# Block products by sevens in a fused attention and feed-forward kernel: the first feed-forward product computed over two token tiles with seven block products, and its rounds re-dealt

## The chip, the cores and the metric

One core of one Trainium2 chip runs the whole program. The metric is device time in microseconds (us); three runs of the kernel before gave 860.07, 860.36 and 865.73 us, so the median is 860.36 us. Everything is float32.

## What is computed

An attention block in which only scores close to the row's maximum survive, and a feed-forward block behind it. Cut to what matters:

```python
# q, k, v: (8 batches, 8 heads, 576 tokens, 64)
scores = q @ k.T / 8
scores = where(scores >= max(scores) - tau, scores, -1e9)
attn   = exp(scores - max) ; attn = attn / (sum(attn) + 1e-9)
x      = heads side by side of (attn @ v)          # (4608 tokens, 512)

h      = x @ w_in                                  # (4608, 1024), "first product"
e      = exp(h - max(h)) ; solu = h * e / (sum(e) + 1e-9)
ln     = (solu - mean) / sqrt(var + 1e-6) * g_ln
out    = ln @ w_out                                # (4608, 512), "second product"
```

## The kernel before, in words

**Slots and rounds.** The attention part is cut into 144 slots (`slots`, `NS`), 18 for each of the 8 batches (`PER`). A slot is 128 query rows of each head of a pair of heads against all 576 keys. Per batch, 16 slots belong to kinds 0 and 1 (four pairs of heads, two slots each) and two to kind 2, the last 64 tokens of each head. One pass of the big `while` loop is a round. Round n issues slot n's scores and, behind them, the later steps of earlier slots and pieces of the feed-forward part. The order of all instructions is written out by hand (`manual_schedule`), so each engine runs its own list strictly in the order in which the program emits it.

**A slot's steps.** `scores` (L472, TensorE) fills two score tiles in PSUM, `s0` and `s1`, with one buffer each: round n+1 can only write them when round n has been read. `maxes` (L494, VectorE) takes the row maxima from PSUM, one instruction for each head. `ramp` (L509, ScalarE) reads the scores from PSUM a last time and writes `w` in SBUF. `exps` (L518, ScalarE) exponentiates `w` and sums it. One round later `normalise` (L525, L526, L528, GpSimd) divides `w`, and `blocks` (L540, VectorE) transposes it into `T` in 32x32 blocks; after two slots DMAs rearrange `T` into `wT` (L549 to L556). Three rounds after the second slot of a pair of heads, `attend_steps` (L582, TensorE) multiplies `wT` with v into a PSUM tile `pv`, and `attended` (L614, ScalarE) copies it into the token tiles `xh` (or `xe` for kind 2).

**A token tile's steps.** When a kind's four pairs of heads are done, two tiles of 128 tokens are ready; kind 2 gives one tile for every two batches, 36 tiles in all. `ff_h` (L647, in the drain after the last slot L637) does the first product in two parts in two rounds, into one PSUM tile `h_ps`, 64 matmul instructions of 64x512 for a tile as the profile counts them. The array is used as four 64x64 quarters at once. Where the row half that adds into a bank changes, a `fence` (L108, a GpSimd memset that waits for TensorE, and that the next matmul waits for) keeps the two apart. Then come `ff_max` (L662, VectorE), `ff_exp` (L671, ScalarE), `ff_mul` (L677, VectorE), `ff_sum` (GpSimd), `ff_stats` (L692 and L693 VectorE, then five small GpSimd instructions L696 to L703), `ff_norm` (L713, ScalarE), `ff_norm2` (L718, VectorE), `ff_swap` (four DMAs, L729), `ff_turn` (L739, VectorE, a transpose into `uT`), and `ff_o` (L752, TensorE, again in two parts in two rounds) into a PSUM tile `o_ps`, copied out by `ff_out` (L767, ScalarE) and stored by `ff_store`.

**PSUM.** Eight banks: the two score tiles hold four, and the other four are two tiles `p0` and `p1`, which `take` hands out by turns to `pv`, `h_ps` and `o_ps`. A product with v and the two feed-forward products thus never share a bank.

**Order in steady state.** A tile's first product takes two rounds, each with a product with v if one is due, and the second product of the tile before takes the next two rounds, without one. While a slot's scores are with VectorE and ScalarE, TensorE works on these. For batches 2 and up q and k arrive untransposed, are scaled by GpSimd, transposed by VectorE (`turn_natural`, L212, called "flip" here) and rearranged by DMA. Within one round a list `begin` runs before the scores, `middle` after `normalise`, and `late` after `blocks`.

Of the kernel before, what the change touches and what calls it, by code (L numbers as in the profile page):

```python
# [8 lines left out]
F32 = mybir.dt.float32  # L9
# [11 lines left out]
def kernel(  # L21
# [61 lines left out]
    seed = const.tile([P, 1], F32, name="seed")  # L83

# [7 lines left out]
    natural = {}  # L92
    ends = {}
# [27 lines left out]
    def load_one(b, hf, nm, queue=None):  # L121
        d = halves.setdefault((b, hf), {})
        hs = slice(4 * hf, 4 * hf + 4)
        src, rows = {"q": (q, ROWS[0]), "k": (k, ROWS[1])}[nm]
        d[nm] = loads.tile([P, 4, 4, D], F32, tag=nm, name=nm)

        parts = [slice(0, 2), slice(2, 4)] if b == 0 and hf == 0 else [slice(0, 4)]
        for x, part in enumerate(parts):
            queue = nc.scalar if nm == "k" and x + 1 < len(parts) else nc.sync
            queue.dma_start(  # L130
                out=d[nm][:, part].rearrange("p h t d -> p h (t d)"),
                in_=src[b, hs, 0:SM, :][part].rearrange("h (p t) d -> p h (t d)", t=4),
            )
            if hf == 0 and x == 0:
                if b not in ends:
                    ends[b] = loads.tile([P, H, D], F32, tag="ends", name="ends")
                load_ends(b, nm, slice(0, 2) if len(parts) > 1 else slice(0, H), queue)
# [6 lines left out]

    def load_qk(b, hf):
        load_one(b, hf, "q")
        load_one(b, hf, "k")
# [43 lines left out]
    def load_natural(i, nm, a):  # L191
        raw = loads.tile([P, 4, 4, D], F32, tag=nm, name=nm)
        natural[i, nm, a] = raw = raw.rearrange("p h t d -> p (h t d)")[:, 0 : NK * D]
        nc.sync.dma_start(out=raw, in_=qk_rows[nm][a, 64 * i : 64 * i + P])
# [69 lines left out]
    def weight_load(x):  # L264
        raw = work.tile(
            [P, 512], I64 if wide else F32, tag=("xh2", "xh3", "uT", "xh1")[x % 4 if x < 15 else 0],
# [9 lines left out]
    def weight_a(x):  # L276

        if not wide:
# [3 lines left out]
            work.tile([P, 512], I32, tag=t, bufs=n, name="em") for t, n in (("ob", 2), ("xe", 1))  # L282
# [68 lines left out]
    def pair(i):  # L351
        if i not in pairs:
            qT = heads.tile([P, S], F32, tag="qT", bufs=6, name="qT")
            pairs[i] = dict(
                qT=qT[:, 0:SM] if i < 2 * NP else qT,
                kT=heads.tile([P, S], F32, tag="kT", name="kT"),
                qe=heads.tile([P, ST], F32, tag="qe", name="qe"),
            )
        return pairs[i]

    def q_item(i, ts=slice(0, 4)):
        src, h0 = source(i)
# [3 lines left out]
        def make(spare, x):  # L366
            for t in range(n):
                turn(
                    spare, x + t, lambda r, y: src["q"][ROWS[r], h0 + y, ts.start + t], swap=True
# [19 lines left out]
    def k_item(i, ts=slice(0, 4)):  # L389
        src, h0 = source(i)  # L390
# [3 lines left out]
        def make(spare, x):  # L394
            for t in range(n):
                turn(spare, x + t, lambda r, y: src["k"][ROWS[r], h0 + y, ts.start + t])
# [9 lines left out]
    def e_item(i):  # L406
        src, h0 = source(i)
# [152 lines left out]
    def attend_steps(key):  # L560
# [3 lines left out]
        unit["y"] = take("pv")  # L564
# [3 lines left out]
        for e in range(2) if kind == 2 else [None]:  # L568
            for m in range(NK):
                for u in range(2):  # L570
                    d, h0 = source(b * NP + (hp if e is None else e + 2 * u))
                    for h in range(2):
# [4 lines left out]
                        else:  # L577
# [11 lines left out]
                            start=m == 0, stop=m == NK - 1,  # L589
# [3 lines left out]
    def attended(key):  # L593
# [13 lines left out]
        else:  # L607
            if hp == 0:
                xh[b, kind] = work.tile(
                    [P, NP, 256], F32, tag=f"xh{(2 * b + kind) % 4}", bufs=1, name="xh"  # L610
# [4 lines left out]
        pairs_free.append(tag)  # L615


# [46 lines left out]
    def ff_exp(t):  # L664
        d = ffn[t]

        starts.append(t)
        tag = "xh1" if rnd > NS and len(starts) % 2 else "u"
        d["u"] = work.tile([P, DFF], F32, tag=tag, bufs=1, name="u")
# [5 lines left out]
    def ff_mul(t):  # L675
        d = ffn[t]
        nc.vector.tensor_tensor(out=d["u"], in0=d["h"], in1=d["u"], op=ALU.mult)  # L677
        pairs_free.append(d["tag"])
# [65 lines left out]
    def ff_o(t, part):  # L744
        d = ffn[t]
        other = len(t) == 3 and t[0] > 1 and t[2]
        if part == 0:
            d["otag"], d["o"] = take("o_ps")
        for m in range(NC * part, NC * part + NC):
            for r in range(2):  # L750
                for z in range(2):
                    nc.tensor.matmul(  # L752
# [331 lines left out]
```

## Time and profile before

| | |
|---|---|
| median of three runs | 860.36 us |
| the profiled execution's own time | 864.95 us |
| its span | 863.2 us |
| granted TensorE clock, mean | 0.981 |
| first slot's scores begin / 30th slot / last slot | 8.4 / 175.1 / 787.6 us |
| last matmul ends (o_ps) | 858.3 us |
| slots 54 to 72, 72 to 90, 90 to 108, 108 to 126 (18 each) | 97.4, 98.9, 99.2, 97.4 us |

An engine's busy share says how much of the span it had an instruction running; it does not say that the engine sets the time. For that one looks at what each engine waited for. The chain of work that ended last runs for 84% of the span through TensorE: 26% second product, 23% + 3% first product, 16% scores, 15% product with v.

### The profile page before, as it was taken

What the parts mean: (1) busy time and instruction counts of PE and PEld (TensorE: products, weight loads), DVE (VectorE), ACT (ScalarE), POOL (GpSimd) and SP (SyncE); (2) the same over time, 40 slices, a digit from 0 to 9 for tenths busy, and PEclk for the clock granted to TensorE, in tenths of its full rate; (3) what the DMA queues carried; (4) which work ended last, traced back from release to release, by engine and by line L of the source; (5) the groups of instructions that cost most, each with busy time, mean ns of one, the idle gap of its engine ahead of it and who ended that gap; (6) DMA issues with size and microseconds to landing.
All of it is one profiled execution on the core that took longest, in us unless ns stands there. A gap on an engine that the chain in (4) does not pass through costs nothing.

```text
span 863.2 us, 36114 instructions
## 1 busy us (share of the span) xinstructions
PE 817.0 (95%) x15361; PEld 634.7 (74%) x15361; DVE 673.5 (78%) x1232; ACT 572.1 (66%) x1153; POOL 495.1 (57%) x936
## 2 busy tenths in 40 slices
PE   4659789999999999999999999999999999999997
PEld 3437567777688888888788886777788888887655
DVE  4987777978788888888788887888888888787361
ACT  5876867777667767777677766767677776775121
POOL 2876756566666656565656655565666655555120
PEclk9878999999999999999999999999999999999999
DMA  9999796997878778888788787888788887555312
GB/s 288 243 254 251 185 203 162 234 248 196 224 196 219 202 196 208 220 214 198 201 202 222 198 194 192 212 222 206 183 228 229 193 196 186 154 141 140 69 38 62
DMA packets 83712, 168.54 MB, mean 195 GB/s; under 512 B 15448, under 2 KB 45152, under 8 KB 83552
## 3 DMA queue, kind: packets, MB, share of 16 engines
q1 hardware_dynamic: 82416, 164.25, 75.5%
q8 instruction: 120, 1.97, 1.0%
q10 hardware_dynamic: 1136, 2.00, 0.7%
q14 instruction: 40, 0.33, 0.1%
HBM read 46.14 MB, written 9.44 MB: 64 GB/s over the span
## 4 chain that ended last, share of the span: by engine, by line
PE 84%; DMA 6%; ACT 4%; issue 2%; DVE 2%; POOL 1%; SPq 1%; ACTq 0%; DVEq 0%
PE o_ps L752 26%; PE h_ps L647 23%; PE s_ps L472 16%; PE pv L582 15%; DMA wT<-T 4%; PE h_ps L637 3%; ACT w L509 1%; ACT w L518 1%; DMA qT<-flip 1%; DMA w<-w 1%; DVE w L494 1%; DMA k<-in_k_dram 1%; ACT qT L374 0%; PE s_ps L337 0%; POOL w L528 0%
## 5 line engine op out<-in xcount | busy, mean ns | idle before, releaser
L752 PE MATMUL o_ps<-w,uT 64*64 64x256 f32 x4608 | 273.1, 376 | 4.3 <-issue 1.9
L494 DVE CUSTOM_DVE_ANT_0 w<-s_ps,tau_t 128x576 f32<-128x576 f32 x280 | 200.0, 751 | 94.4 <-PE s_ps L472 67.0
L509 ACT ACTIVATE w<-s_ps,nth 128x576 f32<-128x576 f32 x280 | 197.0, 739 | 110.8 <-DVE nth L494 90.8
L752 PEld LDWEIGHTS o_ps<-w,uT 64*64 64x64 f32 x4608 | 221.5, 133 | 59.3 <-ACT xh L614 12.0
L528 POOL TENSOR_SCALAR w<-w,sm 128x576 f32<-128x576 f32 x288 | 221.5, 781 | 14.3
L540 DVE STREAM_TRANSPOSE T<-w 128x576 f32<-128x576 f32 x288 | 207.5, 755 | 22.0 <-POOL w L528 20.6
L647 PE MATMUL h_ps<-w,xh 64*64 64x512 f32 x1856 | 223.1, 589 | 0.7 <-issue 0.7
L518 ACT ACTIVATE w<-w,ntau 128x576 f32<-128x576 f32 x288 | 219.8, 768 | 0.0
L582 PEld LDWEIGHTS pv<-wT,v 64*64 64x64 f32 x5760 | 179.7, 137 | 37.4 <-issue 12.8
L472 PE MATMUL s_ps<-kT,qT 64*64 64x512 f32 (+1 forms) x2048 | 177.1, 413 | 14.0 <-ACT w L509 12.0
L582 PE MATMUL pv<-wT,v 64*64 64x128 f32 (+1 forms) x5760 | 179.5, 266 | 9.7 <-DMA wT<-T 7.2
L647 PEld LDWEIGHTS h_ps<-w,xh 64*64 64x64 f32 x1856 | 131.7, 133 | 65.4 <-issue 10.6
L525 POOL TENSOR_SCALAR sm<-sm 128x2 f32<-128x2 f32 x144 | 34.7, 241 | 203.7 <-ACT w L518 200.1
L526 POOL TENSOR_TENSOR sm<-sm,mone 128x2 f32<-128x2 f32 x144 | 105.8, 735 | 12.0
L472 PEld LDWEIGHTS s_ps<-kT,qT 64*64 64x64 f32 x2048 | 76.0, 136 | 21.1 <-ACT w L509 16.4
L614 ACT COPY xh<-pv 128x256 f32<-128x256 f32 x64 | 25.0, 390 | 83.3 <-PE pv L582 83.2
L713 ACT ACTIVATE V<-u,nb,rs 128x1024 f32<-128x1024 f32 x36 | 44.7, 1241 | 39.6 <-POOL nb L703 32.6
L739 DVE STREAM_TRANSPOSE uT<-V 128x1024 f32<-128x1024 f32 x36 | 44.3, 1230 | 15.2 <-DMA V<-u 14.8
L518 ACT ACTIVATION_READ_ACCUMULATOR w<-w,ntau 128x1 f32 x288 | 55.9, 194 | 0.0
L677 DVE TENSOR_TENSOR u<-h_ps,u 128x1024 f32<-128x1024 f32 x36 | 42.8, 1189 | 9.7 <-ACT u L671 9.7
L718 DVE TENSOR_SCALAR u<-u,rs,nb 128x1024 f32<-128x1024 f32 x36 | 35.5, 987 | 17.2 <-ACT V L713 17.1
L662 DVE TENSOR_REDUCE hm<-h_ps 128x1 f32<-128x1024 f32 x36 | 43.0, 1193 | 6.0 <-PE h_ps L647 3.3
(88 smaller groups left out, 562.9 us busy)
## 6 DMA issues: line engine op xcount, KB each, us to landing
wT<-T SPq DMA_DIRECT2D x160, 288.0 KB, 6.2
wT<-T SPq DMA_DIRECT2D x64, 576.0 KB, 5.5
V<-u SPq DMA_DIRECT2D x144, 64.0 KB, 3.4
out_dram<-ob SPq DMA_DIRECT2D x71, 128.0 KB, 2.5
q<-in_q_dram SPq DMA_DIRECT2D x24, 288.0 KB, 6.1
qT<-flip SPq DMA_DIRECT2D x48, 144.0 KB, 3.8
k<-in_k_dram SPq DMA_DIRECT2D x24, 288.0 KB, 5.9
kT<-flip SPq DMA_DIRECT2D x48, 144.0 KB, 4.2
```

The source lines that it names most:

```text
L472: nc.tensor.matmul(out=ps[h][ROWS[y], ks], lhsT=lhsT, rhs=d["kT"][ROWS[h], ks], start=True, stop=True,)
L494: nc.vector.tensor_tensor_reduce(out=w, in0=ps[:, 0:S], in1=(zero if loose else tau_t).to_broadcast([P, S]), scale=1.0, scalar=BIG, op0=AL ...
L509: nc.scalar.activation(out=d["w"][x], in_=d["w"][x] if d["loose"] else d["ps"][x][:, 0:S], func=AF.Prelu, bias=d["nth"][x], scale=-1.0, al ...
L518: nc.scalar.activation(out=w, in_=w, func=AF.Exp, bias=ntau, scale=1.0, accum_out=sm[:, x : x + 1])
L526: nc.gpsimd.tensor_tensor(out=sm, in0=sm, in1=mone, op=ALU.pow)
L528: nc.gpsimd.tensor_scalar(out=w, in0=w, scalar1=sm[:, x : x + 1], scalar2=1.0, op0=ALU.mult, op1=ALU.mult)
L540: nc.vector.transpose(out=T[:, :, r, h, :], in_=w)
L582: nc.tensor.matmul(out=to, lhsT=d["v"][ROWS[u], (h0 + h - u) % 4 if b > 1 else h0 + h, m ^ 4 * u if m < 8 and b < 2 else m,], rhs=rhs, sta ...
L647: mm = nc.tensor.matmul(out=h[ROWS[y], f], lhsT=x[ROWS[r], c, ROWS[y]], rhs=w1_parts[ROWS[r], c, part ^ r], start=part == 0 and c == 0, st ...
L713: nc.scalar.activation(out=V, in_=u, func=AF.Identity, bias=nb, scale=rs)
L739: nc.vector.transpose(out=uT, in_=d["V"].rearrange("p y (m x) -> p m y x", x=32))
L752: nc.tensor.matmul(out=d["o"][ROWS[z], 512 * (r ^ other) : 512 * (r ^ other) + 256], lhsT=d["uT"][ROWS[r], m].rearrange("p y x -> p (y x)" ...
```

## The change

It touches the rounds from 30 on (`START`); the rounds before keep the old way.

* **Seven products.** Two token tiles of one kind are taken together as a 2x2 block matrix (two tiles by two halves of the 512 inputs) and multiplied with the 2x2 blocks of `w_in` by seven block products instead of eight (Winograd's form), which needs sums of token blocks (`sums_a`, `sums_b`, `sum_one`, GpSimd), sums of weight blocks (`seven_weights`, GpSimd, eight of them in rounds 21 to 28) and sums of results.
* **One tile h.** The products go through one PSUM tile for the rest of the program (`both["h"]`, two banks), in seven phases of 8 matmul calls. Between the phases ScalarE copies halves out into SBUF (`keep_half`) and VectorE adds halves from PSUM (`add_half`, which also gives the maximum, so that `ff_max` falls away for these tiles; `pair_exp` combines two maxima and exponentiates from SBUF).
* **v beside o.** The product with v and the second product share the other two banks (`both["o"]`): v in columns 0 to 127 of each bank, o in columns 256 to 511. The product with v no longer starts its sum afresh; after each copy (L609) VectorE sets its columns to zero (`clear`, L617).
* **Turns.** In even rounds, counted from round 30, TensorE does the scores, one phase, the product with v and one more phase (the seventh phase stands alone behind the product with v). In odd rounds it does the scores and half of a second product. A pair's fourteen rounds of jobs are laid down in `new_pair`.
* **Buffers.** q and k are loaded by pairs of heads instead of by four heads into three buffers, the second three hold weight sums afterwards; `u` has three buffers, `xh` two, `ob` one.

The core of the diff:

```diff
     def attend_steps(key):
-        unit["y"] = take("pv")
+        unit["y"] = (None, both["o"]) if "o" in both else take("pv")
...
-                            start=m == 0, stop=m == NK - 1,
+                            start=m == 0 and "o" not in both, stop=m == NK - 1,
...
     def attended(key):
         nc.scalar.copy(out=to, in_=y)
-        pairs_free.append(tag)
+        if tag:
+            pairs_free.append(tag)
+        else:
+            clear()
+
+    def clear():
+        nc.vector.memset(both["o"].rearrange("p (u n) -> p u n", u=2)[:, :, 0:P], 0.0)
+
+    def sums_a(ts):
+        x1, x2 = [tokens(t) for t in ts]
+        both["s"] = work.tile([P, 2, P], F32, tag="sum", bufs=1, name="sum")
+        nc.gpsimd.tensor_tensor(out=both["s"], in0=x2[:, 0:2], in1=x2[:, 2:4], op=ALU.add)
+        nc.gpsimd.tensor_tensor(out=x2[:, 0:2], in0=x2[:, 0:2], in1=x1[:, 0:2], op=ALU.subtract)
+
+    def sums_b(ts):
+        x1 = tokens(ts[0])
+        nc.gpsimd.tensor_tensor(out=x1[:, 0:2], in0=both["s"], in1=x1[:, 0:2], op=ALU.subtract)
+        nc.gpsimd.tensor_tensor(out=x1[:, 2:4], in0=x1[:, 2:4], in1=x1[:, 0:2], op=ALU.subtract)
+
+    PHASES = ((1, 2), (2, 1), (6, 5), (5, 6), (7, 3), (3, 7), (4, 4))
...
+    def phase(ts, k):
+        h = both["h"]
+        last = []
+        for c in range(2):
+            for r, n in enumerate(PHASES[k]):
+                bank = r if n == 4 else n in (2, 3, 5)
+                x, w = product(ts, n, c)
+                for y in range(2):
+                    mm = nc.tensor.matmul(
+                        out=h[ROWS[y], 512 * bank : 512 * bank + 512],
+                        lhsT=x[ROWS[r], ROWS[y]], rhs=w[ROWS[r]],
+                        start=c == 0 and (n, r, k) in ((1, 0, 0), (2, 1, 0), (5, 1, 2), (4, 1, 6)),
+                        stop=c == 1 and k in (1, 3, 5, 6), skip_group_check=True,
+                    )
+                    if k in (1, 3, 5) and not last:
+                        sync(mm, both["fence"])
+                    last.append(mm)
+        if k in (0, 2, 4):
+            both["fence"] = fence(last[-4:])
...
+    def keep_half(t, g, bank):
+        nc.scalar.copy(out=half(ffn[t]["x"], g), in_=half(both["h"], bank))
+
+    def add_half(t, g, bank):
+        ...
+        nc.vector.tensor_tensor_reduce(
+            out=to, in0=half(both["h"], bank), in1=to, scale=1.0, scalar=-BIG,
+            op0=ALU.add, op1=ALU.max, accum_out=m,
+        )
...
+    def new_pair(ts, r):
+        def first():
+            ...
+            keep_half(a, 0, 0)
+            add_half(a, 0, 1)
+            sums_b(ts)
+        def second():
+            ...
+            keep_half(a, 1, 0)
+            keep_half(b, 1, 1)
+        at(late, 1, first)
+        at(late, 3, second)
+        at(late, 5, lambda: (add_half(a, 1, 1), add_half(b, 1, 0), pair_exp(a)))
+        at(late, 6, lambda: (pair_mul(a), ff_sum(a)))
+        at(middle, 7, lambda: ff_stats(a))
+        at(late, 7, lambda: (keep_half(b, 0, 1), add_half(b, 0, 0), pair_exp(b)))
+        at(begin, 8, lambda: ff_norm(a))
+        at(middle, 8, lambda: (ff_norm2(a), ff_swap(a)))
+        at(late, 8, lambda: (pair_mul(b), ff_sum(b)))
+        at(middle, 9, lambda: ff_stats(b))
+        at(late, 9, lambda: ff_turn(a, r + 9))
+        at(begin, 10, lambda: ff_norm(b))
+        at(middle, 10, lambda: (ff_norm2(b), ff_swap(b)))
+        at(late, 14 if r + 14 <= NS else 11, lambda: ff_turn(b, rnd))
...
+        def steady_round(due):
+            if (rnd - START) % 2:
+                o_steps(NC)
+                return
+            if not hsteps and ready and ready[0][0] <= rnd:
+                ts = ready.pop(0)[1]
+                if len(ts) == 2:
+                    new_pair(ts, rnd)
+                    sums_a(ts)
+                    for k in range(0, 7, 2):
+                        hsteps.append([lambda k=k, ts=ts: phase(ts, k)])
+                        if k < 6:
+                            hsteps[-1].append(lambda k=k, ts=ts: phase(ts, k + 1))
+            ...
+            steps = hsteps.pop(0) if hsteps else []
+            if steps[1:] or steps and rnd >= NS:
+                steps[0]()
+            if due:
+                key = pv_due.pop(0)[1]
+                for _ in attend_steps(key):
+                    pass
+                done_with(key)
+            elif rnd >= NS:
+                o_steps(NC // 2 if steps else NC)
+            if steps and rnd < NS or steps[1:]:
+                steps[-1]()
```

`done_with` calls `attended`. In a round, everything shown here is emitted after the round's `maxes`, `ramp`, `exps`, the `normalise` of the round before and the `middle` jobs, and ahead of `blocks` and the `late` jobs. A single tile (kind 2) still takes eight block products (`one_h`), in two even rounds.

## The prediction

> **What bounds the kernel now.** I read the shares of the engines first, then the chain of waits, then one second-product round in order of time. From slot 30 on TensorE is busy to 99% or 100% in every window of 100 us. The chain that ended last, cut to 400 to 416 us, gives what each kind of work costs there (start, length, line, instructions):
>
> ```profile
> 402.34 3.37 PE h_ps L647 x32
> 405.71 1.91 PE pv L582 x70
> 407.72 1.00 PE s_ps L472 x7
> 408.72 3.33 PE o_ps L752 x64
> ```
>
> Half of a tile's first product is 3.37 us, a product with v 1.91, a slot's scores 1.00, half of a second product 3.33. The other engines fit beside it with little to spare; this is a round with a second product, in order of time:
>
> ```profile
> 783.13 1.29 PE L472 MATMUL s_ps<-kT,qe 64*64 64x64 f32 x16
> ...
> 784.45 0.76 DVE L494 CUSTOM_DVE_ANT_0 w<-s_ps,tau_t 128x576 f32<-128x576 f32 x1 [0.43 <-PE s_ps L472]
> ...
> 785.30 1.42 ACT L509 ACTIVATE w<-s_ps,nth 128x576 f32<-128x576 f32 x2 [1.40 <-DVE nth L494]
> 785.81 0.09 DVE L494 DVE_READ_ACCUMULATOR2_ANT nth<- 128x1 f32 x1
> ...
> 787.25 1.38 DVE L540 STREAM_TRANSPOSE T<-w 128x576 f32<-128x576 f32 x2
> ...
> 787.56 1.29 PE L472 MATMUL s_ps<-kT,qe 64*64 64x64 f32 x16
> 788.05 0.19 ACT L518 ACTIVATION_READ_ACCUMULATOR w<-w,ntau 128x1 f32 x1
> ```
>
> Counted from the start of the scores: VectorE takes the maxima from +1.32 to +2.77, ScalarE has read the scores at +3.59, the next scores start at +4.43, the exponentials end at +5.11. So in such a round VectorE may be late by about 0.8 us before TensorE has to wait; in a round with a first product and v (6.4 us) by 2.7. Now it is seldom late:
>
> ```profile
> DVE w L494 <- PE s_ps L472: 67.0, 71, 5.7
> PE s_ps L472 <- ACT w L509: 12.9, 14, 3.1
> ```
>
> VectorE waits 67.0 us for scores, its reserve; TensorE waits 12.9 us for the score tiles. Prices for what follows:
>
> ```profile
> L677 DVE TENSOR_TENSOR u<-h_ps,u 128x1024 f32<-128x1024 f32 x36 | 42.8, 1189 | 9.7 <-ACT u L671 9.7
> L739 DVE STREAM_TRANSPOSE uT<-V 128x1024 f32<-128x1024 f32 x36 | 44.3, 1230 | 15.2 <-DMA V<-u 14.8
> L614 ACT COPY xh<-pv 128x256 f32<-128x256 f32 x64 | 25.0, 390 | 83.3 <-PE pv L582 83.2
> L767 ACT COPY ob<-o_ps 128x512 f32<-128x512 f32 x35 | 19.9, 568 | 9.7 <-PE o_ps L752 9.7
> ```
>
> **What the seven products save.** A pair's first products take 56 matmul calls for 64. Eight calls are half a half: 3.37 / 2 = 1.69 us a phase, and one is saved for each of 14 pairs: 23.6 us of TensorE.
>
> **What VectorE is made to wait for.** In an even round the list of ScalarE holds the copy of v behind both exponentials, and the list of VectorE holds the zeroing behind that copy and ahead of the two block transposes. The product with v is done early, at +4.6, but the copy cannot start before the exponentials end, +5.11; it ends at 5.11 + 0.09 + 0.39 = 5.59. The zeroing has no row: the least is a GpSimd memset of one column (0.10), the most a VectorE copy of 128x256 from PSUM (0.42); I take 0.30, nearer to the copy, as it writes the same 256 columns. It ends at +5.98. Queued behind it: the transposes (1.40), the round's late jobs, the next round's maxima. From the first maximum of an even round to that of the next even round VectorE therefore needs at least (5.98 - 1.32) + 1.40 + 1.36 (odd round's maxima) + 1.40 (its transposes) = 8.8 us, plus late jobs. An add of a half is priced from the maximum (0.68 for 576 columns, so 0.6 for 512 and its accumulator: 0.63; bounds 0.55 and 0.72); the joined maximum 0.15; the multiply 1.15 as now; statistics 1.50; turn 1.23; flip 0.75. A pair's jobs fall into four units of two rounds, r being the pair's first round:
>
> - rounds r+6, r+7: turn 1.23 and multiply 1.15, then statistics 1.50, add 0.63, joined maximum 0.15, flip 0.75: 8.8 + 5.4 = 14.2
> - r, r+1 (with the pair before's leftovers): multiply 1.15, statistics 1.50, turn 1.23, add 0.63: 13.3
> - r+2, r+3: flip 0.75: 9.6, under TensorE's own 6.30 + 4.35 = 10.65
> - r+4, r+5: two adds, joined maximum, flip, 2.2: 11.0
>
> The second normalising pass (about 1.0) lies in the wait for the copy of v and costs nothing there.
>
> **What TensorE is made to wait for.** There is one h tile, so phases 1, 3, 5 and the next pair's first wait in the round after an odd one for what read the banks. Phase 5 waits for two copies of halves (0.57 each) that stand behind the odd round's exponentials: 5.11 + 0.1 + 1.14 + 0.1 = +6.45, where TensorE is ready at 4.43 + 0.99 = 5.42: 1.0 us. A pair's first phase waits for copy and add alike: 1.1. Phase 3 waits for GpSimd: statistics end with VectorE 1.25 us late at 2.77 + 1.25 + 1.50 = 5.5, five small instructions (1.95 in this trace) and two sums (0.65 each by half of the 1.28 us that a 128x512 sum takes) end at 8.9, against 5.95 by then: 2.9 us. Only the last falls in a unit that TensorE sets: 10.65 + 2.9 = 13.55. The others run while VectorE is late anyway.
>
> A pair's eight rounds: 14.2 + 13.3 + 13.55 + 11.0 = 52.1 us. Now eight rounds take 97.4 x 8 / 18 = 43.3.
>
> **The sum.** Rounds 0 to 29 stay at 175.1 us. Rounds 30 to 143 hold 13 pairs' rounds and three single tiles of four rounds each, for which the same count gives about 27 us (reduction 1.2, multiply and flips in place of adds): 13 x 52.1 + 3 x 27 = 758; less the last pair's unit beyond round 143 (14.2) and some 7 us because the first pair has no leftovers before it: 737 us. Now they take 792.0 - 175.1 = 617. After round 143, 64 us of matmuls remain, with waits of about 12: behind the turn of the pair before (3.8), phase 3 (2.3), the last tile's own chain (4.6) and small ones. After the last matmul 4.9 us, as now (863.2 - 858.3). 175 + 737 + 76 + 5 = 993 us of span; the profiled execution's own time is 1.75 above its span and 4.6 above the median, so 990 us.
>
> Loads by pairs of heads, the weight sums on GpSimd in rounds 21 to 28 (8 x 1.28 us, one a round, where GpSimd is busy to 60%) and SyncE's queue, whose swap DMAs move with their jobs, I cost at nothing: GpSimd's free 40% hides them. Without that cover it is 10 us, inside the range.
>
> **The rivals.** *Zeroing costs no wait.* If the copy of v got in early, the chain is 5.9 us a unit and only TensorE's waits on the one h tile are left: units of 11.3, 10.65 + 1.1, 10.65 + 2.3 and 10.65 + 1.0, 47.6 for eight rounds. 13 x 47.6 + 3 x 24 - 16 = 675, and the whole 927 us. For it: copies of v now wait 83 us for TensorE, so ScalarE is usually early. Against: the exponentials stand ahead of it in the list. Chance 0.15.
>
> *TensorE stays the bound, and it is faster.* Place: the even round; price: 23.6 us less three odd rounds without a second product, in which scores alone wait for ScalarE (3.6 us instead of 1.0, 8 us): 845 us. It decides if VectorE starts an odd round's maxima no more than 0.8 us late, which needs zeroing by +4.7, ahead of the exponentials' end. For it: VectorE's busy time fits, about 88 us in 18 rounds of 94. Against: the list. Chance 0.04; another 0.02 for an even split of both.
>
> *The clock falls.* In the first 100 us TensorE was busy for 68.6 us and the granted clock was 0.86; in the steady part it will be busy to some 80%. At 0.9 the 10.65 and 6.3 us rounds grow by a tenth, but half of the units are VectorE's: about 20 us more, 1010 us. [...] By that rule the waits above, at most 2.9 us, leave the sum as it is, and I give this 0.03.
>
> That the change doesn't do what it says is excluded: the changed program issues seven groups of 8 calls a pair.
>
> **How the numbers follow.** The chance of the forecast is 0.76. Cheap ends (zeroing 0.10, add 0.55, quicker turn and multiply) take off 18 us, a hidden wait of phase 3 another 38: 934. Dear ends (zeroing 0.42, add 0.72, sums 0.9) add 18; that rounds now run 2% over the sum of their matmuls (97.4 for 95.2) adds 15: 1023. Its own range is 934 to 1023; with the first rival and the clock, 915 to 1030. A change under 1% cannot be told from none here. Faster 0.04, within 1% 0.02, slower 0.94.
>
> **What would show it.** VectorE's zeroing (L617) should stand behind idle time released by ScalarE's copy (L609), 2 us or more in most even rounds; TensorE's phases (L693) should wait for VectorE, GpSimd and ScalarE; 18 slots should take 114 to 120 us; TensorE's share should fall below 80%. I am wrong if zeroing waits little, if TensorE stays at 95%, or if 18 slots stay under 100 us.

## The result, and the profile after

The changed kernel takes 1060.25 us (median of 4 runs, 1057.53 to 1062.47) against 860.72 us for the kernel before in the same comparison: a ratio of 1.2301, 95% interval 1.2245 to 1.2357. Slower was right; the forecast of 990 us was 70 us short, and the time lies outside the range.

The page of the changed kernel, TensorE's share and the groups that the prediction priced (busy us, mean ns of one, idle time ahead of them and what ended it):

```profile
PE 880.5 (83%) x15329; PEld 563.2 (53%) x15329; DVE 689.5 (65%) x1403; ACT 598.1 (56%) x1209; POOL 557.5 (53%) x1022
...
L617 DVE MEMSET ov<- 128x256 f32 x60 | 16.3, 272 | 225.8 <-ACT xh L609 172.4
```

Its waits (engine and line, what it waited for, us in total, times, longest):

```profile
ACT w L503 <- DVE nth L488: 223.0, 88, 8.0
DVE ov L617 <- ACT xh L609: 172.4, 47, 7.2
ACT xh L609 <- PE ov L576: 65.6, 36, 4.4
DVE w L488 <- PE s_ps L466: 49.8, 49, 5.4
PE ov L576 <- DMA wT<-T: 44.2, 44, 2.7
PE h L693 <- DVE hm L739: 35.5, 22, 2.7
```

VectorE no longer waits for scores first of all (67.0 us before, 49.8 now), but 172 us for ScalarE's copy of v, and ScalarE in turn 223 us for VectorE's maxima. This is the wait that the prediction describes, though ahead of the copy there often stands another: ScalarE's copy of v was itself released by TensorE's product with v in 36 places (65.6 us). One even round and the odd round behind it, in order of time (TensorE, VectorE and ScalarE; the bracket is idle time and its releaser):

```profile
437.28 1.95 PE L693 MATMUL h<-w,xh 64*64 64x512 f32 x16 [0.54 <-POOL mark L110]
437.79 0.19 ACT L512 ACTIVATION_READ_ACCUMULATOR w<-w,ntau 128x1 f32 x1
437.88 0.37 ACT L609 COPY xh<-ov 128x256 f32<-128x256 f32 x1
438.38 0.27 DVE L617 MEMSET ov<- 128x256 f32 x1 [1.77 <-ACT xh L609]
438.56 1.40 DVE L534 STREAM_TRANSPOSE T<-w 128x576 f32<-128x576 f32 x2
...
440.99 0.75 DVE L488 CUSTOM_DVE_ANT_0 w<-s_ps,tau_t 128x576 f32<-128x576 f32 x1
...
444.68 0.57 ACT L732 COPY u<-h 128x512 f32<-128x512 f32 x1
445.20 1.20 DVE L934 STREAM_TRANSPOSE uT<-V 128x1024 f32<-128x1024 f32 x1
446.33 0.65 DVE L739 CUSTOM_DVE_ANT_0 u<-h,u 128x512 f32<-128x512 f32 x1
...
447.14 1.12 PE L693 MATMUL h<-k,xh 64*64 64x512 f32 x2 [2.51 <-DVE hm L739]
```

The copy of v (437.88) follows the read of the last exponential's sum here, as predicted; of the 56 even rounds from 32 on that is so in 17, with zeroing waiting 1.9 us on average, and in the other 39 (copies into `xe` counted in) the product with v ended later and zeroing waited 4.5 us. Zeroing follows the copy, the transposes and a multiply follow zeroing, and the odd round's maxima begin only at 440.99. Then the next even round's third phase waits 2.51 us for VectorE's add, which stands behind the turn. What the prediction did not have is what follows. Windows of 3.41 us around that wait (length, busy us and instructions of TensorE, its weight loads, VectorE, ScalarE and GpSimd, granted clock, DMA share, GB/s):

```profile
440.19:443.60 3.41, 3.41 (x76) 2.44 (x69) 3.41 (x7) 1.76 (x3) 2.12 (x3) 1.00 0.78 179
443.60:447.01 3.41, 1.03 (x20) 0.15 (x12) 3.38 (x8) 2.17 (x6) 2.61 (x7) 1.00 0.72 187
447.01:450.42 3.41, 3.28 (x16) 1.16 (x20) 2.90 (x6) 3.23 (x6) 3.14 (x5) 0.50 0.44 91
450.42:453.83 3.41, 3.41 (x92) 2.51 (x88) 0.58 (x2) 1.28 (x5) 2.86 (x7) 1.00 0.52 152
```

In 443.60 to 447.01 TensorE works 1.03 of 3.41 us; in the next 3.41 us its clock is granted at 0.50, and 16 instructions fill a window in which 76 or 92 ran. Such windows all begin on one grid of 3.413 us in a trace. Behind 165 us the changed kernel has 35 of them, the kernel before one. At a clock of 0.50 a stretch of 3.41 us takes up to 1.71 us of TensorE's work away, by half of its length; in runs 6 and 12 below the same 64 instructions took 5.37 us with such a window and 3.69 without, 1.68 us apart. Half of the time that TensorE was busy in those 35 windows is 53 us, against a miss of 70.

### The profile page after: what moved, and what is told of

Same layout as the page of the kernel before. It is cut to its first block, busy times and chain, and to the rows that moved or that the text cites. A ratio compares the mean times of both kernels' runs of the same rounds, so it can differ in the third digit from the quotient of the medians.

```text
span 1060.7 us, 36434 instructions
## 1 busy us (share of the span) xinstructions
PE 880.5 (83%) x15329; PEld 563.2 (53%) x15329; DVE 689.5 (65%) x1403; ACT 598.1 (56%) x1209; POOL 557.5 (53%) x1022
## 4 chain that ended last, share of the span: by engine, by line
PE 29%; DVE 22%; DMA 17%; issue 13%; ACT 11%; POOL 4%; SPq 3%; DVEq 0%; ACTq 0%; POOLq 0%
DMA wT<-T 13%; PE h L693 10%; PE ov L576 7%; DVE T L534 6%; DVE w L488 5%; PE s_ps L466 5%; ACT w L503 3%; PE o_ps L950 3%; ACT w L512 3%; DVE bs L887 2%; DVE u L739 2%; ACT V L908 2%; DMA v<-in_v_dram 2%; PE h_ps L843 2%; PE pv L576 2%
## 5 line engine op out<-in xcount | busy, mean ns | idle before, releaser
L488 DVE CUSTOM_DVE_ANT_0 w<-s_ps,tau_t 128x576 f32<-128x576 f32 x282 | 200.7, 748 | 53.5 <-PE s_ps L466 49.8
L576 PE MATMUL ov<-wT,v 64*64 64x128 f32 (+1 forms) x4752 | 165.1, 288 | 60.0 <-DMA wT<-T 44.2
L576 PEld LDWEIGHTS ov<-wT,v 64*64 64x64 f32 x4752 | 150.7, 153 | 111.5 <-issue 35.1
L950 PE MATMUL ov<-w,uT 64*64 64x256 f32 x3456 | 200.0, 377 | 8.7 <-DVE uT L934 8.7
L466 PE MATMUL s_ps<-kT,qT 64*64 64x512 f32 (+1 forms) x2048 | 173.3, 426 | 16.3 <-ACT w L503 15.3
L950 PEld LDWEIGHTS ov<-w,uT 64*64 64x64 f32 x3456 | 144.1, 133 | 77.4 <-issue 31.7
L617 DVE MEMSET ov<- 128x256 f32 x60 | 16.3, 272 | 225.8 <-ACT xh L609 172.4
L693 PE MATMUL h<-w,xh 64*64 64x512 f32 x896 | 115.1, 611 | 30.0 <-POOL mark L110 13.5
L693 PEld LDWEIGHTS h<-w,xh 64*64 64x64 f32 x896 | 37.5, 135 | 83.2 <-issue 24.6
L891 POOL TENSOR_SCALAR rs<-mv,se 128x1 f32<-128x1 f32 x36 | 12.8, 356 | 129.3 <-DVE mv L888 129.2
L950 PE MATMUL o_ps<-w,uT 64*64 64x256 f32 x1152 | 71.3, 394 | 11.1 <-DVE uT L934 8.3
L693 PE MATMUL h<-sums,xh 64*64 64x512 f32 x336 | 70.3, 697 | 0.4 <-DVE hm L739 0.4
L693 PE MATMUL h<-k,sum 64*64 64x512 f32 x224 | 69.6, 749 | 0.0
L950 PEld LDWEIGHTS o_ps<-w,uT 64*64 64x64 f32 x1152 | 48.4, 140 | 37.7 <-issue 17.3
```

The lines of the kernel that those rows point to most:

```text
L466: nc.tensor.matmul(out=ps[h][ROWS[y], ks], lhsT=lhsT, rhs=d["kT"][ROWS[h], ks], start=True, stop=True,)
L488: nc.vector.tensor_tensor_reduce(out=w, in0=ps[:, 0:S], in1=(zero if loose else tau_t).to_broadcast([P, S]), scale=1.0, scalar=BIG, op0=AL ...
L576: nc.tensor.matmul(out=to, lhsT=d["v"][ROWS[u], (h0 + h - u) % 4 if b > 1 else h0 + h, m ^ 4 * u if m < 8 and b < 2 else m,], rhs=rhs, sta ...
L693: mm = nc.tensor.matmul(out=h[ROWS[y], 512 * bank : 512 * bank + 512], lhsT=x[ROWS[r], ROWS[y]], rhs=w[ROWS[r]], start=c == 0 and (n, r, k ...
L950: nc.tensor.matmul(out=d["o"][ROWS[z], of : of + 256], lhsT=d["uT"][ROWS[r], m].rearrange("p y x -> p (y x)"), rhs=w2[ROWS[r], m ^ r, 256 ...
```

## The experiments

Theory Z: VectorE's wait for the copy of v, ahead of zeroing, sets the rounds. Rival H: TensorE's waits on the one h tile set them. Rival D: the loop zeroing, T, transfer of wT, product with v. Theory C, formed after the first runs and estimated from windows like the one at 443.60 above (1.03 of 3.41 us busy): a wait that takes more than about half of one 3.41 us window from TensorE costs half the clock in the next. Runs 1 to 8 were timed once each, so that differences of a few us between them say little; the kernel before took 863.81 us beside the first four.

**1. Zeroing moved to the start of the next round.**

```diff
 def attended(key):
-            clear()
+            begin.setdefault(rnd + 1, []).append(clear)
```

> The zeroing of the v columns is moved from behind the copy of v to the start of the next round, ahead of that round's maxima; nothing else changes. Theory Z (VectorE's wait for the copy of v sets the rounds; the halved clock comes on top): the wait of VectorE for the copy falls from 225.8 us to under 60 us, eight rounds fall from 54 to 55 us to 49 to 51, the whole to 970 to 1010 us. Theory H (TensorE's waits on the one h tile and the clock that halves behind them set the rounds): 1040 us or more. Theory D (the loop through the wT transfer sets them): 1040 or more as well, with the waits of v's products for the transfer at 60 us as now.

978.49 us. 82 us of the 200 lost are won back by moving one instruction of 0.27 us. The waits of this kernel:

```profile
DVE w L488 <- PE s_ps L466: 115.7, 81, 6.7
DVE ov L617 <- ACT xh L609: 46.9, 29, 4.8
PE ov L576 <- ACT ob L968: 25.5, 15, 2.7
PE h L693 <- DVE hm L739: 25.0, 21, 2.0
PE ov L576 <- DMA wT<-T: 12.0, 15, 2.4
```

Zeroing waits 47 us where it waited 172, and VectorE waits for scores again (116 us). TensorE still waits 25 us for the add, where it waited 35.5, so H does not account for the gain; the waits for the transfer fell from 44 to 12 us along with the time, so D, which expected them to stay and the time too, falls. The halved windows behind 165 us fall from 35 to 14, and half of TensorE's busy time in them from 53 to 20 us: up to 33 of the 82 us can be the clock, the rest goes with the wait.

**2. No zeroing at all.**

```diff
-    start=m == 0 and "o" not in both, stop=m == NK - 1,
+    start=m == 0, stop=m == NK - 1,
...
-        else:
-            clear()
```

> No zeroing at all; each product with v starts its sums afresh, which also makes a second product lose its first half where a product with v falls between its halves. Theory Z: within 15 us of the kernel that zeroes a round later, as the instruction itself (60 x 0.27 = 16 us of VectorE) is not the point but the wait. If it is more than 30 us below, the waits of the second product for the zeroing in its bank count as well.

975.28 us, 3 us from run 1. So it is the place of the zeroing, not its 0.27 us or its work, that costs.

**3. The h tile emptied earlier, zeroing left in place.**

```diff
-        at(late, 1, first)
-        at(late, 3, second)
+        at(begin, 1, lambda: sums_b(ts))
+        at(soon(1), 1, first)
+        at(soon(3), 3, second)
+        at(soon(5), 5, lambda: (add_half(a, 1, 1), add_half(b, 1, 0)))
...
```

`soon(n)` is a new list that runs between `ramp` and `exps`; `first` no longer holds `sums_b`.

> The copies and adds of the halves of h move from behind an odd round's exponentials to between its score reads and its exponentials, and the two late sums of token blocks on GpSimd to the start of the round; the zeroing stays. TensorE's waits for phases 3, 5 and the next first phase should go. Theory Z: no gain, 1040 to 1090 us, because VectorE still waits for the copy of v and what TensorE waited for h it now waits for wT. Theory H: the halvings behind phase 3 go, eight rounds fall by the 2.5 us of wait and 1.7 us of halved clock, the whole to 990 to 1010 us.

1094.76 us: not faster by H's amount but 34 us slower than the changed kernel, a little past Z's range too. The waits:

```profile
DVE ov L617 <- ACT xh L609: 174.4, 50, 8.1
PE ov L576 <- DMA wT<-T: 42.7, 48, 2.8
PE h L694 <- POOL mark L110: 39.0, 12, 4.3
```

The wait for the add is gone and another stands in its place: GpSimd's one-column write that fences the phases now waits behind what was put ahead of it, 3.3 us each of 12 times. The zeroing waits as before, and the halved windows rise from 35 to 42. As TensorE went on waiting for h, this run alone does not settle H; with run 1, where the time fell while most of the wait for the add stayed, H does not set the rounds by itself.

**4. Both.** The edits of runs 1 and 3 together.

> Both edits: zeroing a round later, and copies, adds and late sums earlier. Theory Z with little interplay: the same as zeroing a round later alone or a little above, 970 to 1015 us, since the fence on GpSimd and the wT transfer take over. If the two add up (each hides part of the other), 930 us or less.

1022.38 us, a little past Z's range: 72 us better than run 3, about what zeroing's place is worth, and 44 us worse than run 1. The two edits do not add up, and the fence's wait is here too (46.2 us in 13 waits).

The next four runs had the kernel before at 867.03 us.

**5. Zeroing added to the kernel before.**

```diff
 def attended(key):
         nc.scalar.copy(out=to, in_=y)
+        nc.vector.memset(whole, 0.0)
         pairs_free.append(tag)
```

> The kernel before with one thing added: VectorE zeroes v's columns of a tile right behind ScalarE's copy of v out of it, as the changed kernel does; the product with v still starts afresh, so the zeroing is work without use, and all eight block products stay. Theory Z (the place of the zeroing in VectorE's list sets the rounds): the zeroing waits 2 to 4 us in most rounds with v, 18 rounds take 105 to 118 us where they take 96 now, and the whole 950 to 1000 us. Rival (the zeroing is harmless as long as TensorE has other work to do): at most 20 us above before.

982.25 us, 115 us slower by one useless instruction per product with v. 18 slots take 110 to 118 us (five stretches from slot 36 on). Its order of time shows the zeroing's wait without anything else of the change:

```profile
504.38 0.77 ACT L518 ACTIVATE w<-w,ntau 128x576 f32<-128x576 f32 x1
505.05 0.19 ACT L518 ACTIVATION_READ_ACCUMULATOR w<-w,ntau 128x1 f32 x1
...
506.12 0.40 ACT L614 COPY xh<-pv 128x256 f32<-128x256 f32 x1 [0.87 <-PE pv L582]
506.64 0.27 DVE L615 MEMSET pv<- 128x256 f32 x1 [3.32 <-ACT xh L614]
506.82 1.40 DVE L540 STREAM_TRANSPOSE T<-w 128x576 f32<-128x576 f32 x2
508.14 0.74 DVE L212 STREAM_TRANSPOSE flip<-q 128x576 f32<-128x576 f32 x1
508.80 0.72 DVE L494 CUSTOM_DVE_ANT_0 w<-s_ps,tau_t 128x576 f32<-128x576 f32 x1
```

VectorE stands still for 3.32 us and then has two transposes, a flip and the next maxima to do. The copy itself waits here for the product with v (0.87 us), not for the exponentials. Theory Z holds: it is the place behind the copy that costs, whatever the copy waits for.

**6. Twelve waits put into the kernel before.** The second product of every other tile of rounds 44 to 139 waits for the round's last read of the scores.

```diff
+    if part == 0 and m == r == z == 0 and 44 <= rnd < 140 and turns.index(t) % 2:
+        sync(mm, live[rnd]["read"])
```

> The kernel before with one wait added: the second product of every other tile in rounds 44 to 139, twelve in all, does not begin before ScalarE has read that round's scores (2.3 us after them by the trace of before), so that TensorE stands idle for about 2.6 us twelve times. Work and results are unchanged. If a wait costs only its own length: 12 x 2.6 = 31 us, about 892 us, granted clock over the whole run as before. Theory C (after such a wait the clock is granted at half for 3.4 us): up to 12 x 1.7 = 20 us more, about 905 to 915 us, and stretches at half clock behind the waits in the trace.

907.61 us. The waits are 2.20 to 2.48 us, 28.8 us in all, and nine of the twelve are followed by a window at half clock: 28.8 + 9 x 1.71 = 44.1 us, and the span grew by 905.8 - 863.2 = 42.6. Three were not, though they are as long (2.20, 2.46 and 2.20 us). The windows on this trace's grid, a wait of 2.46 us ahead of 420.18, one of 2.20 ahead of 469.04 and one of 2.46 ahead of 514.93:

```profile
417.35:420.76 3.41, 0.95 (x16) 0.46 (x16) 2.92 (x7) 3.00 (x6) 1.50 (x4) 1.00 0.88 223
420.76:424.17 3.41, 3.41 (x40) 2.13 (x36) 1.67 (x2) 0.88 (x4) 2.25 (x4) 0.50 0.94 238
465.13:468.55 3.42, 1.70 (x40) 0.82 (x29) 2.69 (x6) 2.47 (x5) 2.28 (x4) 1.00 0.97 295
468.55:471.96 3.41, 2.92 (x56) 2.11 (x60) 2.74 (x4) 1.95 (x5) 1.18 (x3) 1.00 1.02 277
512.92:516.33 3.41, 1.40 (x28) 1.02 (x32) 3.41 (x7) 2.99 (x8) 0.81 (x2) 1.00 0.87 213
516.33:519.75 3.42, 3.42 (x68) 2.18 (x64) 0.98 (x3) 0.07 (x1) 2.42 (x4) 1.00 0.97 229
```

The same wait falls whole into one window (0.95 of 3.41 us busy, 28%: halved) or is cut by a border of the grid (50% and 41% busy: not halved). Behind 165 us of this trace windows 27% to 35% busy were followed by half clock, windows of 41% and more were not.

**7. The eighth group of calls put back.** The last phase runs twice.

```diff
-    hsteps.append([lambda k=k, ts=ts: phase(ts, k)])
+    hsteps.append([lambda k=k, ts=ts: [phase(ts, k) for _ in range(1 + (k == 6))]])
```

> The changed kernel with the last of the seven block products computed twice into the same banks: an eighth group of 8 calls for each pair, so that TensorE has the same work as before (the output differs by that product). Theory Z: TensorE waits in that round anyway, so the time stays within 10 us of the changed kernel's 1060. If TensorE's own work still bounded these rounds: 14 x 1.69 = 24 us more, 1084 us.

1068.19 us, 8 us more than the change and not 24 (2 us more, if each is set against the kernel before beside it, 867.03 and 860.72). The work that the seven products save lies mostly beside waits. It is not a clean difference: this run has 32 halved windows behind 165 us for 35.

**8. Jobs in other places.** Zeroing next round; copies of halves in `begin`, adds behind the maxima, sums and turn moved, fences on VectorE, the last phase ahead of v's product, the second tile's turn earlier.

```diff
-        at(late, 1, first)
-        at(late, 3, second)
+        at(begin, 1, first)
+        at(soon(1), 1, lambda: add_half(a, 0, 1))
+        middle.setdefault(r + 1, []).insert(0, lambda: sums_b(ts))
+        at(begin, 3, second)
...
-            both["fence"] = fence(last[-4:])
+            both["fence"] = fence(last[-4:], nc.vector)
```

> The changed kernel with its jobs in other places, same arithmetic: zeroing at the start of the next round (as in the first run); copies of halves at the start of a round, ahead of the scores' reads; adds right behind the maxima; GpSimd's second pair of sums at the head of the middle list, its first at the end of a round; the one-column writes that fence the phases on VectorE instead of GpSimd; the last phase ahead of v's product; the second tile's turn ahead of the exponentials of round r+14. Theory Z with the one h tile (H) as second limit and half clock behind each wait: with the waits gone the time falls by 150 us or more against the changed kernel, to 885 to 930 us. If something else sets the rounds (the loop over the transfer of wT, for one): above 960 us.

944.5 us: 116 us better than the change, between the two expectations, and still 9% above before. Its waits:

```profile
DVE ov L618 <- ACT xh L610: 50.5, 35, 3.9
PEld ov L958 <- DVE ov L618: 31.5, 24, 3.0
PE ov L577 <- DMA wT<-T: 21.4, 29, 1.5
PE ov L577 <- ACT ob L976: 17.9, 9, 2.5
```

TensorE stands idle for 64 us in rounds 30 to 143, where it was 133 us in the changed kernel and 3 us in the kernel before. The largest of TensorE's waits left are those of v and o, which share their banks: the second product waits for the zeroing, v for the transfer and for the copy of o. That the shared banks are the reason was not tested by a run. No order that was run brings the changed program near 860 us.

**9 and 12. The waits of run 6, with TensorE working in them.** The first calls of the second product run ahead of the waiting one and are done over.

```diff
+    for i in range(24):
+        mi, ri, zi = i // 4, i // 2 % 2, i % 2
+        nc.tensor.matmul(
+            out=d["o"][ROWS[zi], 512 * (ri ^ other) : 512 * (ri ^ other) + 256],
+            lhsT=d["uT"][ROWS[ri], mi].rearrange("p y x -> p (y x)"),
+            rhs=w2[ROWS[ri], mi ^ ri, 256 * zi : 256 * zi + 256],
+            start=mi == 0, stop=mi == 5,
+        )
     mm = nc.tensor.matmul(
```

Run 12 has 12 calls for 24.

> The kernel before with the same twelve waits as in the run before_gaps (second products wait for the round's score read, 2.20 to 2.48 us each), but TensorE no longer idle in them: the first 24 matmuls of that second product run ahead of the waiting one and are then done over (about 1.25 us; the waits end at the same moments, the results are the same). There nine of the twelve waits were followed by 3.41 us at half clock. Theory C (the clock is set anew every 3.41 us by how much TensorE worked in the 3.41 us before, and halves when that is under about 45%): TensorE works 60% and more of each such stretch, no halved stretch follows, and the time falls by 9 x 1.7 = 15 us, to about +25 us over the kernel before. Rival (the waits themselves cost 40 us): +40 us as there.

> As gaps_filled, whose 24 matmul calls took 2.8 us, twice what was reckoned (a call is two instructions), and so left no wait at all: now 12 calls, 1.4 us, so that about 1.0 us of each of the twelve waits stays and they end when they ended in the run before_gaps. Theory C: no stretch at half clock, 12 x 2.4 = 29 us over the kernel before, about 890 to 893 us, against 41 us over it with the waits unfilled. Rival (the waits themselves cost 41 us, whatever TensorE does in them): 41 us over it again, 900 to 908 us.

Run 9: 896.86 us, ratio 1.0365 (1.0283 to 1.0446), more than the 25 us expected: a call is two instructions in the profile, so the fill took 2.8 us and left no wait, and none of these places halved. Run 12: 896.45 us, ratio 1.0370 (1.0299 to 1.0441); that is 31 us over the kernel before beside it, where 29 were expected (the time itself is 3 us above the range of 890 to 893, and clear of the rival's 900 to 908). TensorE at the same place in run 6 and then in run 12:

```profile
416.56 1.16 PE L472 MATMUL s_ps<-kT,qT 64*64 64x64 f32 x16
420.18 5.37 PE L752 MATMUL o_ps<-w,uT 64*64 64x256 f32 x64 [2.46 <-ACT w L509]
```

```profile
415.92 1.16 PE L472 MATMUL s_ps<-kT,qT 64*64 64x64 f32 x16
416.90 1.48 PE L755 MATMUL o_ps<-w,uT 64*64 64x256 f32 x24
419.54 3.69 PE L761 MATMUL o_ps<-w,uT 64*64 64x256 f32 x64 [1.17 <-ACT w L509]
```

The wait ends 3.62 us behind the start of the scores in both, but the same 64 instructions behind it take 3.69 us and not 5.37. Run 12 has no halved window behind 165 us while TensorE works. From the end of the first wait to the end of the twelfth, run 6 takes 521.84 us and run 12 508.14: 13.70 us, which is 8 x 1.71, the halved windows in between. In the kernel before, theory C is shown here: the waits alone cost about 29 us, the clock the rest.

**10, 11 and 13. The same tried in the changed kernel.** Matmuls without use into unused columns of o's banks, ahead of phases and products with v.

```diff
+        def fill():
+            for i in range(32):
+                r, z = i // 2 % 2, i % 2
+                nc.tensor.matmul(
+                    out=both["o"][ROWS[z], 512 * r + P : 512 * r + 256],
+                    lhsT=w2[ROWS[r], 0, 0:64], rhs=w2[ROWS[r], 0, 0:P],
+                    start=False, stop=False, skip_group_check=True,
+                )
```

Run 11 has 16 calls in two places of each pair, run 13 eight calls there, into the first bank and with the first 64 rows alone.

> The changed kernel with 32 matmuls without use (128 columns each, into columns of o's banks that nobody reads, about 0.9 us by the product with v's rate) ahead of each round's phase of the first product and again ahead of each product with v, rounds 30 to 143; it only adds work, about 100 us of TensorE's time in all, and takes no wait away. Theory C: much of it runs while TensorE waits for VectorE, GpSimd, ScalarE or a DMA; the stretches at half clock, 35 of 3.41 us after 165 us in the changed kernel, fall to 12 or fewer, and the time falls although work was added, to 1010 to 1045 us. If halved clock is a symptom that costs nothing (TensorE would wait anyway): no fall, 1060 us or more.

> The changed kernel with 16 matmul calls without use (0.9 us by the product with v's rate: 72 instructions, two a call, in 1.95 us) in two places of each pair alone, those after which its trace shows most of the stretches at half clock: ahead of the third phase (round r+2, waits about 2.6 us for VectorE or GpSimd) and ahead of the product with v in round r+6 (waits 2 to 2.7 us for the transfer of wT). About 30 fills, 27 us of work, nearly all inside waits that stay as long as they end now. Theory C: TensorE then works 50% to 60% of those 3.41 us where it worked 20% to 40%, most of the halved stretches there go, 35 after 165 us become 15 or fewer, and the time falls by 15 to 40 us to 1020 to 1045 us although work was added. Rival (half clock is a by-product that costs nothing, as VectorE sets the rounds): the same time or up to 27 us more, 1060 to 1087 us, also with fewer halved stretches.

> As two_waits_filled (the changed kernel with matmuls without use ahead of the third phase and ahead of the product with v in round r+6), but with 8 calls into columns 128 to 255 of o's first bank alone, which the copy out of o does not span: there the fills waited 142 us for that copy, which was a new wait and no test. About 29 fills of about 0.9 us, in waits of 2 to 2.7 us. Theory C: TensorE works half of those 3.41 us, the stretches at half clock after 165 us fall from 35 to 18 or fewer, and the time falls by 15 to 35 us against the changed kernel, to 1025 to 1045 us (ratio to before 1.19 to 1.215), though work was added. Rival (half clock costs nothing here, as VectorE sets the rounds): as many fewer stretches, but 1055 us or more (ratio 1.225 and above).

1148.85 us (ratio 1.3290, 1.3206 to 1.3374), 1073.99 us (1.2436, 1.2363 to 1.2509) and 1083.57 us (1.2544, 1.2459 to 1.2630). By time all three miss what theory C expected, and each lies where its rival, that half clock costs nothing here, put it. But none is a test between the two: the fills brought a wait of their own, and the halved windows did not go as expected. In run 11:

```profile
PE ov L1133 <- ACT ob L968: 59.4, 26, 4.1
```

The fill waits for ScalarE's copy of o out of the bank (the 142 us that the expectation of run 13 names add the waits of the fill's weight loads, 82.3 us, to this one), in run 13 too (58.6 us), where the columns of the two do not overlap but the bank is the same. In run 10 a fill also took 1.93 us, not 0.9. Halved windows behind 165 us: 18, 28 and 37, where 12, 15 and 18 at most were expected. No bank of the eight is free of a reader, and no run changes the clock alone in the changed kernel itself; what it costs there is read from its own trace below.

## Why the prediction was right or wrong

**Right: where VectorE loses its time.** The zeroing takes 0.272 us (taken: 0.30) and waits for the copy of v 172 us in 47 rounds, 3.7 us each (test: 2 us or more). Runs 1, 2 and 5 show that its place decides. Why the copy is late was right in part only: "the copy cannot start before the exponentials end, +5.11" puts it at +5.2, and it starts 5.2 to 10.8 us behind the start of the scores, in 39 of 56 rounds because the product with v ended last. That product stands behind phases that wait, so TensorE's waits and its clock reach VectorE through the copy; the prediction had the product done at +4.6 and left this path out. The first rival's 47.6 us for eight rounds, with zeroing free, is nearly what run 1 takes, though zeroing waits 47 us there: 47.8 to 49.8 for each of the nine pairs from slot 58 to 138. Its 927 us was not met (978), as the first pairs, the last rounds and halved windows cost there as well.

**Right in size, in part by luck: the units.** From the starts of the scores in the changed kernel's trace, each pair's eight rounds from slot 50 to 138, by the number of halved windows in them (us):

| unit | predicted | none halved | one halved |
|---|---|---|---|
| r, r+1 | 13.3 | 12.5 to 14.2, mean 13.4 (9) | 15.9 (1) |
| r+2, r+3 | 13.55 | 12.9 to 13.9, mean 13.1 (4) | 15.1 to 15.8, mean 15.4 (6) |
| r+4, r+5 | 11.0 | 11.3 to 12.8, mean 12.0 (10) | |
| r+6, r+7 | 14.2 | 13.1 to 13.3, mean 13.2 (3) | 14.6 to 16.2, mean 15.3 (5) |

Two units r+6 held two halved windows (17.4 and 15.6). The units without a halved window add up to 13.4 + 13.1 + 12.0 + 13.2 = 51.7 us for a pair, where 52.1 was predicted; they are also those with the shorter waits. Taking half of TensorE's busy time in the halved windows off each of the ten pairs from slot 50 to 138 leaves 51.7 to 53.1, 52.4 us on average. Errors cancel in it: a GpSimd sum takes 0.72 to 1.07 us (taken: 0.65), the copy starts later than predicted, the unit r+6 is shorter than its sum, r+4 longer. Phase 3's wait was put at 2.9 us, for GpSimd's sums. It is 2.5 to 3.0 us in seven of the ten pairs, but in five of these VectorE's add came last, so that the size was partly luck; behind single tiles (slots 52, 88 and 124) it is 0.75, and the second phase of these pairs waited 3.1 us for the fence, which the prediction did not have.

**Wrong: the clock.** The step that failed is the third rival: "By that rule the waits above, at most 2.9 us, leave the sum as it is, and I give this 0.03", and its price, "about 20 us more". No trace or run shows a rule by which waits of this length leave the clock as it is. What the runs showed in its place: in every trace the halved stretches begin on one grid of 3.413 us, and waits of 2.20 to 2.48 us, with TensorE 27% to 35% busy in the window, were followed by half clock nine times out of twelve in run 6. So the prediction passed over phase 3's wait (round r+2), which it had itself put at 2.9 us; the wait of v's product for the transfer of wT in round r+6, 1.6 to 2.7 us, it did not have at all. These two rounds hold 13 of the 15 stretches at half clock from slot 60 on; the other two belong to single tiles. The other half of the argument, that "half of the units are VectorE's" and slow matmuls lie beside them, failed too, by units with equal waits. Units r+2 whose third phase waits 2.5 to 2.7 us take 15.1 to 15.4 us with one halved window (slots 60, 68, 104 and 132) and 13.9 without (slot 112). Units r+6 whose product with v waits 1.6 to 1.8 us take 14.6 and 14.7 with one (slots 108 and 136) and 13.1 to 13.3 without (64, 72 and 100). So a halved window costs 1.2 to 1.6 us here; the means of the table lie 2.1 to 2.3 apart because the halved units held the longer waits as well. In run 5, where VectorE's zeroing delays the rounds too, units with the same wait of 2.45 us take 13.5 us without and 15.2 with one (slots 72, 112 and 136): 1.7 us. In slot 112 of the changed kernel a border of the grid cut the wait of 2.66 us ahead of 751.95; TensorE was busy for 56% and 66% of the two windows, and no halved one followed:

```profile
747.39:750.80 3.41, 1.90 (x32) 0.75 (x22) 3.38 (x6) 2.64 (x6) 1.69 (x6) 1.00 0.97 255
750.80:754.22 3.42, 2.27 (x36) 1.31 (x40) 3.09 (x8) 2.92 (x5) 3.07 (x5) 1.00 0.55 162
```

**The sum again.** Rounds 30 to 143 take about 799 us (predicted 737). 31 halved windows lie in them, and half of TensorE's busy time there is 47 us of the miss of 62; about 7 of the rest lie in the first two pairs, 3 in the single tiles (27.9 us each for 27). From there to the end it is 91 us for 81, with four more halved windows, 6 us; the head is 4.6 us shorter. 62 + 10 - 4.6 = 67 of the 68 us by which the span, 1060.7, passes the 993 worked out. Against the kernel before, the same rounds lost 182 us: TensorE is idle in them for 133 us where it was for 3, and half clock takes the 47. If all of the 53 us lies on the path, the changed kernel would take about 1007 us at full clock, inside the range of the forecast; that is worked out, not shown by a run of its own.

**Tests.** VectorE's zeroing behind the copy and TensorE's phases behind VectorE, GpSimd and ScalarE: as said. The five stretches of 18 slots from slot 54 on take 122.5 to 126.5 us (said: 114 to 120); with half of the busy time in halved windows taken off, 117 to 121. TensorE's share is 83% (said: under 80%). Work at half clock counts as busy for longer (the 64 instructions of run 12 took 3.69 us, in run 6 5.37), so that a busy share hides part of the loss; but with that part (69 us over the whole trace) taken off both the busy time and the span, the share is still 82%, so this test failed for another reason too, which stays open. The 23.6 us of the seven products: by run 7 some 16 of them lie beside waits. Loads, weight sums and SyncE's queue were put at nothing: none of them is among the waits shown, and no run tests them.

## What to carry to other kernels

An instruction of a quarter of a microsecond costs what it waits for and what is queued behind it on its engine (the zeroing of 0.27 us cost 115 us in run 5, and moving it won back 82 in run 1): ask of each added step which list it stands in, and put it where its condition has long been met. Where TensorE is nearly full, price a wait twice: its length, and the half clock that came behind nine of the twelve waits of run 6 (1.71 us each by run 12) and cost 1.2 to 1.6 us in the changed kernel. For waits of 2.2 to 2.7 us it was a matter of where they fell on a grid of 3.413 us, and that grid began elsewhere in each trace (borders 0.58 us behind the start of the span in run 3, 2.50 in run 5, 3.29 in run 12). Two results that share a bank shared their waits in this program, even in columns that do not touch (58.6 us in run 13).

## What the runs showed of the hardware that was not expected

- Seen on that grid, the granted clock of TensorE was full or half in a window (1.00 or 0.50), never between, and which of the two went with TensorE's work in the window before. Counted in windows at full clock behind the first 10 us, TensorE busy for 40% and less was always followed by half clock. Between 41% and 57% both occurred (42% in the window at 236.10 of run 3, then full clock; 56% at 168.19 of run 1, then half); the 45% named ahead of run 9 was the author's estimate and lies in this band. Above that half clock came only in run 13, five times, after 60% to 63% busy; in four of these windows the filling matmuls ran, which used the first 64 rows alone, in the fifth (172.1) they did not. No run shows what decides there.
- A window at half clock was followed by another one whenever TensorE was busy in it for less than 79%; between 79% and 94% both occurred (80% at 641.58 of the changed kernel, then full clock; 94% at 40.83, then half), and above that full clock always came back.
- The rounds of the changed kernel fell in with the grid: a pair's eight rounds mostly take 54 to 55 us, and 16 windows are 54.6 us, so that phase 3's wait meets the same place of the grid pair after pair (halved windows begin at 447.0 and 501.6, at 641.6 and 696.2, at 890.8 and 945.4, each time 54.6 us apart).
